# An attention and two-MLP kernel: three elementwise steps change their engine

## The chip, the cores and the metric

One core of one Trainium2 chip runs the kernel. The metric is device microseconds (us) from the first to the last instruction of an execution; lower is better. The engines of a core are TensorE (PE in the profile; PEld is its weight load), VectorE (DVE), ScalarE (ACT), GpSimd (POOL) and SyncE (SP), which here issues the DMAs.

## What is computed

Causal attention with a learned decay, then an MLP with a squared relu, then an MLP with a leaky relu:

```
scores = q @ k.T / 8 + (cum[query] - cum[key]);  masked where key > query
attn   = softmax(scores) @ v            # 4 batches, 8 heads, 576 positions, head size 64
h = x @ w_in   (2304 x 512 @ 512 x 2048)
x1 = (s * relu(h)**2 + b) @ w_out       # first MLP
h2 = x1 @ w_in2
out = max(0.01 * h2, h2) @ w_out2       # second MLP
```

`cum` is the running sum of log f. The weights arrive as float64.

## The kernel before

Products are made in float32r from two halves: an operand is split into a high half, rounded to float32r, and a low half, the rest; three products (high by high, high by low, low by high) replace one. So an MLP block of 128 hidden columns is 12 matmuls of 256 columns for `h` and 12 for the output sums in the first MLP, and 12 and 12 of 512 columns in the second.

The work is staged in nine units of 256 tokens. Units 0 to 7 are a batch's first 256 queries (units 0 to 3, "light" attention: two tiles of queries per head) or its next 256 (units 4 to 7, "heavy": two tiles per head, and a half tile of 64 queries for each pair of heads); unit 8 is the 4 x 64 queries left over. A unit's first MLP runs together with the attention of the next unit, in "slots" laid between its 16 blocks. A prologue makes the first unit's attention and converts the first weights. Then comes the second MLP in five chunks of up to 512 tokens, 16 blocks each; its weights are converted during unit 8 and the first chunk (lines 102 to 106 and 111 to 112: ScalarE, three VectorE steps, ScalarE, GpSimd).

A scheduler turns the program text into one order for each engine; every engine then takes its own instructions strictly in that order, and a waiting instruction holds those behind it. The DMAs that matter here all stand in SP's one queue.

The steps that the change touches:

- **The score of a tile** (`st_score`): two matmuls (four or more for a half tile) into `ps_s`; line 337 on VectorE adds the decays `cumk` (a row of cum, sent by DMA to all partitions, two buffers) and takes the least; line 351 on ScalarE is the exponential. Behind it: line 372 and 373 split the weights into `p_hl` (two buffers), a DMA transposes that to `p_t`, and line 394 multiplies with v.
- **The causal mask** (`st_mask`, line 296): GpSimd writes a large negative number over the diagonal block of `cumk`, after its DMA has landed and before line 337 reads it. It is emitted one tile ahead. Where a light head's two tiles stand side by side, `cumk` is loaded a second time behind itself.
- **g of the first MLP** (`mlp1_g`): line 711 relu, PSUM (`ps_h`, two banks) to SBUF (`graw`), and line 712 square, both ScalarE; line 713 the high half, GpSimd; line 714 the low half, VectorE. The output products (line 733) need both. The bank of `ps_h` is free after line 711.
- **g of the second MLP** (`mlp2_h`): line 798 on ScalarE makes 0.01 h, line 799 on VectorE the maximum with h, line 800 (VectorE) the high half, line 801 (VectorE) the low half. `ps_h` has four banks by then.

## Time and profile before

| | us |
|---|---|
| median of 3 runs | 1104.73 (1100.14 to 1105.5) |
| the profiled execution: span | 1104.1 |
| TensorE busy | 1004.9 (91%) |
| VectorE busy | 710.0 (64%) |
| ScalarE busy | 445.5 (40%) |
| GpSimd busy | 342.0 (31%) |

The profile gives no time for that execution beside its span; the span lies between the lowest and the median run. Matmuls are pipelined, so a TensorE that is busy 91% of the time isn't 91% at its peak: its real load has to be worked out from columns. The shares are averages over stages: the prologue and unit 0 up to about 150 us, units 1 to 6 with attention beside them up to about 600 us, units 7 and 8 up to about 700 us, and the second MLP.

### The profile page before, as it was taken

The numbers are of one execution on the slowest core, as the hardware profiler recorded it, in microseconds if no ns is written. First come the engines' busy times: TensorE is split into PE (matmuls) and PEld (weight loads), VectorE is DVE, ScalarE is ACT, GpSimd is POOL, SyncE is SP. The second block draws the span as 40 slices with busy tenths as digits, with TensorE's granted clock in tenths as the row PEclk, the third lists the DMA queues.
The fourth block names the chain that finished last, engine by engine and source line by source line (L and its number), as shares of the span: only waits on it lengthen the run. The fifth ranks groups of instructions, "written<-read, shape, count | busy, mean of one in ns | idle before, by whom it ended". The sixth has DMA issues, their size and how long they took to land.

```text
span 1104.1 us, 18869 instructions
## 1 busy us (share of the span) xinstructions
PE 1004.9 (91%) x6600; PEld 884.5 (80%) x6600; DVE 710.0 (64%) x1682; ACT 445.5 (40%) x1074; POOL 342.0 (31%) x591
## 2 busy tenths in 40 slices
PE   6876798889899988898989999899999999999998
PEld 4676687888888878787889999767888888888887
DVE  6788977776887877787765159998523533433343
ACT  4555566554555655555554235433101111111111
POOL 4344566644454444454431225433000000000000
PEclk9998989999999999999999999999999999999999
DMA  7388555469898998888874055450200010010010
GB/s 271 125 201 242 154 129 101 98 156 170 171 196 183 211 180 159 197 176 176 187 133 117 8 192 191 124 200 1 77 1 1 20 39 1 1 39 1 0 39 20
DMA packets 191791, 129.32 MB, mean 117 GB/s; under 512 B 137872, under 2 KB 167056, under 8 KB 191696
## 3 DMA queue, kind: packets, MB, share of 16 engines
q1 hardware_dynamic: 191696, 128.12, 48.2%
q8 instruction: 52, 0.85, 0.3%
q14 instruction: 43, 0.35, 0.1%
HBM read 86.58 MB, written 10.04 MB: 88 GB/s over the span
## 4 chain that ended last, share of the span: by engine, by line
PE 47%; DMA 17%; DVE 16%; issue 10%; POOL 6%; ACT 2%; SPq 1%; POOLq 0%; DVEq 0%; ACTq 0%
PE ps_o L809 16%; PE ps_h L791 15%; DMA p_t<-p_hl 7%; PE ps_o L733 6%; PE ps_h L688 6%; DMA cumk<-cumd 4%; DMA qk_raw<-in_qk 3%; DVE wt L104 2%; DVE tt L337 2%; POOL w L112 2%; DVE wt L106 1%; DVE p_hl L373 1%; DVE g L714 1%; POOL g L713 1%; PE ps_v L394 1%
## 5 line engine op out<-in xcount | busy, mean ns | idle before, releaser
L688 PE MATMUL ps_h<-x,w 128*128 128x256 f32 x1728 | 264.3, 288 | 13.2 <-POOL w L112 7.9
L733 PE MATMUL ps_o<-g,w 128*128 128x256 f32 (+1 forms) x1536 | 237.3, 292 | 16.5 <-POOL g L713 9.8
L688 PEld LDWEIGHTS ps_h<-x,w 128*128 128x128 f32 x1728 | 235.1, 194 | 17.1 <-POOL w L112 8.9
L733 PEld LDWEIGHTS ps_o<-g,w 128*128 128x128 f32 x1536 | 206.1, 193 | 27.2 <-POOL g L713 14.3
L809 PE MATMUL ps_o<-w,g 128*128 128x512 f32 x864 | 215.6, 396 | 5.2 <-DVE g L800 3.6
L791 PE MATMUL ps_h<-x,w 128*128 128x512 f32 (+1 forms) x960 | 211.0, 368 | 0.0
L809 PEld LDWEIGHTS ps_o<-w,g 128*128 128x128 f32 x864 | 159.7, 188 | 46.4 <-DVE g L800 6.3
L791 PEld LDWEIGHTS ps_h<-x,w 128*128 128x128 f32 x960 | 169.1, 188 | 32.1
L799 DVE TENSOR_TENSOR t<-ps_h,t 128x512 f32<-128x512 f32 (+1 forms) x80 | 50.8, 635 | 176.7 <-ACT t L798 176.4
L798 ACT ACTIVATE t<-ps_h 128x512 f32<-128x512 f32 (+1 forms) x80 | 44.3, 554 | 279.3 <-PE ps_h L791 279.3
L714 DVE TENSOR_TENSOR g<-graw,g 128x256 fp32r<-128x256 f32 x128 | 70.0, 549 | 66.0 <-POOL g L713 65.9
L351 ACT ACTIVATE tt<-tt,sm 128x512 f32<-128x512 f32 (+4 forms) x128 | 76.8, 600 | 88.3 <-DVE sm L337 79.3
L327 PE MATMUL ps_s<-k_st,q_st 128*128 128x288 f32 (+4 forms) x352 | 91.8, 335 | 20.3 <-DVE sm L337 10.1
L373 DVE SCALAR_TENSOR_TENSOR p_hl<-tt,sm,p_hl 128x512 f16<-128x512 f32 (+4 forms) x128 | 87.5, 692 | 22.5 <-ACT p_hl L372 21.4
L372 ACT ACTIVATE p_hl<-tt,sm 128x512 f16<-128x512 f32 (+4 forms) x128 | 73.5, 596 | 60.3 <-DMA p_t<-p_hl 46.5
L112 POOL TENSOR_TENSOR w<-wt,w 128x512 fp32r<-128x512 f32 x48 | 68.1, 1421 | 79.4 <-ACT w L111 77.8
L296 POOL TENSOR_SCALAR_AFFINE_SELECT cumk<-cumk 128x128 f32<-128x128 f32 (+2 forms) x120 | 46.9, 392 | 137.4 <-DMA cumk<-cumd 99.1
L394 PE MATMUL ps_v<-p_t,v_st 128*128 128x128 f16 (+1 forms) x912 | 60.5, 214 | 27.0 <-DMA p_t<-p_hl 23.8
L327 PEld LDWEIGHTS ps_s<-k_st,q_st 128*128 128x128 f32 x352 | 59.1, 194 | 26.6 <-DVE sm L337 15.1
L713 POOL TENSOR_SCALAR g<-graw 128x256 fp32r<-128x256 f32 x128 | 63.4, 497 | 50.7 <-ACT graw L712 41.1
L337 DVE CUSTOM_DVE_ANT_0 tt<-ps_s,cumk 128x512 f32<-128x512 f32 (+4 forms) x128 | 63.2, 497 | 23.5 <-POOL cumk L296 18.7
L394 PEld LDWEIGHTS <-v_st 128*128 128x128 f16 x912 | 46.8, 100 | 36.7 <-issue 15.8
(88 smaller groups left out, 1116.8 us busy)
## 6 DMA issues: line engine op xcount, KB each, us to landing
w_raw<-in_moe_w_in SPq DMA_DIRECT2D x32, 512.0 KB, 5.4
w_raw<-in_moe_w_out SPq DMA_DIRECT2D x32, 512.0 KB, 5.3
qk_raw<-in_qk SPq DMA_DIRECT2D x32, 480.0 KB, 4.5
cumk<-cumd SPq DMA_DIRECT2D x32, 256.0 KB, 4.3
qk_raw<-in_qk SPq DMA_DIRECT2D x24, 256.0 KB, 3.9
x1d<-x1o SPq DMA_DIRECT2D x36, 128.0 KB, 2.4
cumk<-cumd SPq DMA_DIRECT2D x32, 144.0 KB, 3.5
v_raw<-in_v SPq DMA_DIRECT2D x16, 288.0 KB, 4.2
```

What stands on the lines that cost most here:

```text
L112: nc.gpsimd.tensor_tensor(w[:, 1], x, w[:, 0].bitcast(F32), ALU.subtract)
L327: nc.tensor.matmul(o, q_st[j + e][:, q0 - u0 : q0 - u0 + P], k_st[j + e][:, a, k0 : k0 + kw], start=(e == 0 and a == 0), stop=(e == ne - 1 ...
L337: nc.vector.tensor_tensor_reduce(tt[:, at + k0 : at + k0 + kw], o, cumk[jb][:, at + k0 : at + k0 + kw], scale=-SCALE, scalar=3.0e38 if c = ...
L351: nc.scalar.activation(e, e, AF.Exp, bias=sm[:, r : r + 1], scale=-1.0, accum_out=sm[:, 2 + r : 3 + r])
L373: nc.vector.scalar_tensor_tensor(v[:, 1, :w], e, inv, v[:, 0, :w], ALU.mult, ALU.subtract)
L394: nc.tensor.matmul(av[:, at + e * m : at + (e + 1) * m], v_st[j + e][:, k].rearrange("p l d -> p (l d)"), pt[:, to + l * nk + k, e * m : ( ...
L688: nc.tensor.matmul(ps, wi[:, a, d * P : (d + 1) * P], x[:, c, d], start=(d == 0 and n == 0), stop=(d == ND - 1 and n == 2),)
L713: nc.gpsimd.tensor_scalar(g[:, 0, :UN], raw, 1.0, 0.0, ALU.mult, ALU.add)
L714: nc.vector.tensor_tensor(out=g[:, 1, :UN], in0=raw, in1=g[:, 0, :UN].bitcast(F32), op=ALU.subtract)
L733: nc.tensor.matmul(po[d], wo[:, a, d * P : (d + 1) * P], g[:, c], start=(first and n == 0), stop=(last and n == 2),)
L791: nc.tensor.matmul(ps[:, :n], wi[:, a, d * P : (d + 1) * P], x[:, e, d, :n], start=(d == 0 and k == 0), stop=(d == ND - 1 and k == 2),)
L809: nc.tensor.matmul(po[m], g[:, a, m * P : (m + 1) * P], wo[:, e, :], start=(i == 0 and k == 0), stop=(i == NF - 1 and k == 2),)
```

## The change

Three things are changed together:

- `mlp1_g`: relu and square are done in place in PSUM, and the high half is a ScalarE copy from PSUM. GpSimd has no part in it any more, `graw` is gone, and line 714 (704 after) reads PSUM. The bank of `ps_h` is free only after that.
- the causal mask: an identity matrix times a constant mask block (both bf16, made once in the prologue) is added to the scores by one more matmul per tile (line 317 after). `st_mask` is gone, so is the second load of `cumk` for light heads; `load_cumk(jb + 2)` is emitted behind the tile's line 337.
- `mlp2_h`: leaky relu by one ScalarE activation in place in PSUM, the high half by a ScalarE copy; VectorE keeps the low half, from PSUM.

```diff
-            for at, n in ((0, kend), (kend, P))[: 1 + (u0 == 0)]:
-                nc.sync.dma_start(
-                    out=cumk[jb][rows, at : at + n],
...
+            nc.sync.dma_start(
+                out=cumk[jb][rows, :kend],
...
-    def st_mask(i):
...
+                if end:
+                    nc.tensor.matmul(o[:, kw - m :], ident_h, mask_l if half else mask_h, start=False, stop=True)
                 nc.vector.tensor_tensor_reduce(
                     tt[:, at + k0 : at + k0 + kw],
                     o,
-                    cumk[jb][:, at + k0 : at + k0 + kw],
+                    cumk[jb][:, k0 : k0 + kw],
...
+        if last:
+            load_cumk(jb + 2)
...
-            st_mask(i + 1)
...
+    nc.gpsimd.memset(mask_l, 0.0)
+    for e in range(2):
+        nc.gpsimd.affine_select(
+            out=mask_l[e * D : (e + 1) * D],
...
-        raw = gp.tile([P, UN], F32, tag="raw", name="graw")
...
-        nc.scalar.activation(raw, ps, AF.Relu)
-        nc.scalar.activation(raw, raw, AF.Square)
-        nc.gpsimd.tensor_scalar(g[:, 0, :UN], raw, 1.0, 0.0, ALU.mult, ALU.add)
-        nc.vector.tensor_tensor(out=g[:, 1, :UN], in0=raw, in1=g[:, 0, :UN].bitcast(F32), op=ALU.subtract)
+        nc.scalar.activation(ps, ps, AF.Relu)
+        nc.scalar.activation(ps, ps, AF.Square)
+        nc.scalar.copy(g[:, 0, :UN], ps)
+        nc.vector.tensor_tensor(out=g[:, 1, :UN], in0=ps, in1=g[:, 0, :UN].bitcast(F32), op=ALU.subtract)
...
-        tmp = m2.tile([P, CH], F32, tag="t2", name="t2")
         g = m3.tile([P, 2, CH], F32R, tag="g2", name="g2", bufs=3)
-        raw = tmp[:, :n]
-        nc.scalar.activation(raw, ps[:, :n], AF.Copy, scale=0.01)
-        nc.vector.tensor_tensor(out=raw, in0=ps[:, :n], in1=raw, op=ALU.max)
-        nc.vector.tensor_copy(g[:, 0, :n], raw)
+        raw = ps[:, :n]
+        nc.scalar.activation(raw, raw, AF.Lrelu)
+        nc.scalar.copy(g[:, 0, :n], raw)
         nc.vector.tensor_tensor(out=g[:, 1, :n], in0=raw, in1=g[:, 0, :n].bitcast(F32), op=ALU.subtract)
```

The scheduler moves instructions with it. First GpSimd's queue among the heavy heads (before: L296 is the mask, L713 the high half of g, L242 and L243 split a head's queries, L260 and L371 clear tails, L275 splits v):

```order
L713 TENSOR_SCALAR g<-graw 128x256
L275 TENSOR_SCALAR v_hl<-v_raw,vs 128x5x128
L296 AFFINE_SELECT cumk<-cumk 128x128
L260 MEMSET v_raw 128x64
L296 AFFINE_SELECT cumk<-cumk 128x128
L713 TENSOR_SCALAR g<-graw 128x256
L296 AFFINE_SELECT cumk<-cumk 128x128
L242 TENSOR_SCALAR q_st<-qk_raw 128x384
L243 TENSOR_TENSOR q_st<-qk_raw,q_st 64x384
```

After, in the same stage (L244 and L245 split the queries, L262 and L356 clear tails, L274 and L277 are of v, L409 scales the left-over queries):

```order
L274 TENSOR_SCALAR vs<-vs 128x1
L277 TENSOR_SCALAR v_hl<-v_raw,vs 128x5x128
L244 TENSOR_SCALAR q_st<-qk_raw 128x384
L245 TENSOR_TENSOR q_st<-qk_raw,q_st 64x384
L262 MEMSET v_raw 128x64
L409 TENSOR_SCALAR x_raw<-x_raw,vs 128x64
```

Nothing that a matmul of the first MLP waits for stands in this queue any more, and no instruction in it waits for `cumk`.

Second, TensorE's order of the first MLP beside heavy heads (before: L688 fills `ps_h`, L733 makes the output sums from g, L327 are scores). The g named 4207 is of the `ps_h` named 4194:

```order
L688 MATMUL ps_h_4194<-x_2548,w_1037 128x256
L733 MATMUL ps_o_3535<-g_4139,w_1769 128x256 x6
L733 MATMUL ps_o_3536<-g_4139,w_1769 128x256 x6
L688 MATMUL ps_h_4259<-x_2548,w_1117 128x256 x11
L327 MATMUL ps_s_4750<-k_st_4496,q_st_4495 128x384
L688 MATMUL ps_h_4259<-x_2548,w_1117 128x256
L327 MATMUL ps_s_4750<-k_st_4496,q_st_4495 128x384
L688 MATMUL ps_h_4375<-x_2548,w_1154 128x256 x3
L327 MATMUL ps_s_4819<-k_st_4665,q_st_4664 128x512
L688 MATMUL ps_h_4375<-x_2548,w_1154 128x256
L327 MATMUL ps_s_4819<-k_st_4665,q_st_4664 128x512
L688 MATMUL ps_h_4375<-x_2548,w_1154 128x256 x2
```

After (L680 fills `ps_h`, L724 the output sums, L308 scores, L317 the mask):

```order
L724 MATMUL ps_o_2534<-g_2776,w_1541 128x256 x5
L724 MATMUL ps_o_2535<-g_2776,w_1541 128x256 x5
L680 MATMUL ps_h_2866<-x_1580,w_896 128x256 x12
L724 MATMUL ps_o_2534<-g_2806,w_1634 128x256
L724 MATMUL ps_o_2535<-g_2806,w_1634 128x256
L308 MATMUL ps_s_3588<-k_st_3435,q_st_3434 128x512 x2
L317 LDWEIGHTS ident_h_74
L317 MATMUL ps_s_3588<-mask_h_75,ident_h_74 128x128
L724 MATMUL ps_o_2534<-g_2806,w_1634 128x256 x5
L724 MATMUL ps_o_2535<-g_2806,w_1634 128x256 x5
```

Before, a block of `ps_h` was often begun while two older blocks still lacked their output products; after, blocks of `ps_h` and output products mostly alternate, one block ahead.

Third, ScalarE's queue among heavy heads, before (L711 relu, L712 square, L372 a tile's normalised weights, which wait for the `p_hl` buffer, L351 exponential, L413 output of attention):

```order
L711 ACTIVATE graw_4140<-ps_h_4126 128x256
L712 ACTIVATE graw_4140<-graw_4140 128x256
L372 ACTIVATE p_hl_4469<-tt_4426,sm_4427 128x384
L372 ACTIVATE p_hl_4537<-tt_4483,sm_4484 128x512
L351 ACTIVATE tt_4616,sm_4617<-tt_4616,sm_4617 128x576
L413 COPY x_raw_4326<-ps_v_4401 64x64
```

After (L702 relu, L703 square, L704 the high half, L357 the normalised weights):

```order
L702 ACTIVATE ps_h_5240<-ps_h_5240 128x256
L357 ACTIVATE p_hl_5565<-tt_5522,sm_5523 128x384
L703 ACTIVATE ps_h_5240<-ps_h_5240 128x256
L704 CAST g_5253<-ps_h_5240 128x256
L357 ACTIVATE p_hl_5628<-tt_5579,sm_5580 128x512
L336 ACTIVATE tt_5701,sm_5702<-tt_5701,sm_5702 128x576
```

The high half of g now stands in the queue that also holds the attention's activations, and at this place a wait for a `p_hl` buffer stands between a block's relu and its square.

## Rows read from the trace of the kernel before

The kernel's names in the rows: `g`, `graw`, `ps_h`, `ps_o` are of the MLPs, `ps_s`, `cumk`, `tt`, `sm`, `p_hl`, `p_t`, `ps_v`, `qk_raw` of the attention, `w`, `wt`, `w_raw` of the weights.

**Rows 1.** Windows, all engines: stretch, length, each engine's busy us (instructions), clock, DMA.
```profile
150.00:600.00 450.00, 397.46 (x3464) 374.65 (x3464) 338.92 (x948) 251.74 (x642) 210.24 (x397) 0.97 0.79 163
...
600.00:651.28 51.28, 51.28 (x433) 51.28 (x432) 12.61 (x31) 17.93 (x46) 11.01 (x50) 1.00 0.23 74
...
651.28:763.49 112.21, 104.36 (x581) 86.68 (x579) 107.86 (x153) 51.10 (x96) 51.63 (x44) 1.00 0.46 154
```

**Rows 2.** TensorE by form, 150 to 600 us, first and last of nine.
```profile
L733 PE MATMUL ps_o<-g,w 128*128 128x256 f32 x1152 | 183.3, 294 | 13.9 <-POOL g L713 8.4 <-DVE g L714 4.0 <-DVE x1o L749 0.8
...
L327 PE MATMUL ps_s<-k_st,q_st 128*128 128x256 f32 x22 | 5.2, 294 | 1.1 <-DVE k_st L245 1.1
```

**Rows 3.** Windows, lines 688 and 733 alone, 651.28 to 763.49 us.
```profile
651.28:763.49 112.21, 18.77 (x139) 17.32 (x139) 1.00 0.46 154
...
651.28:763.49 112.21, 24.87 (x170) 21.80 (x168) 1.00 0.46 154
```

**Rows 4.** Waits, 150 to 600 us: us in total, times, longest.
```profile
PE ps_v L394 <- DMA p_t<-p_hl: 20.3, 22, 2.2
PE ps_s L327 <- DVE sm L337: 9.1, 9, 2.4
PE ps_o L733 <- POOL g L713: 8.4, 9, 2.4
PE ps_o L733 <- DVE g L714: 4.0, 9, 0.9
...
DVE g L714 <- POOL g L713: 26.1, 31, 2.3
DVE tt L337 <- POOL cumk L296: 18.4, 17, 3.1
...
POOL cumk L296 <- DMA cumk<-cumd: 85.1, 47, 5.1
...
ACT p_hl L372 <- DMA p_t<-p_hl: 45.1, 37, 3.5
```

**Rows 5.** The chain that ended last, 150 to 600 us, by line.
```profile
by line: DMA p_t<-p_hl 16.9%; issue 13.3%; DMA cumk<-cumd 9.9%; PE ps_o L733 9.0%; DMA qk_raw<-in_qk 6.8%; PE ps_h L688 6.2%; DVE tt L337 4.1%; DVE g L714 3.2%; PE ps_v L394 3.1%; DVE p_hl L373 3.0%; POOL g L713 2.1%; DVE k_st L245 1.9%; PO
```

**Rows 6.** Timeline near 405 us: start, us, instruction, [idle before <- releaser].
```profile
405.26 0.29 POOL L296 TENSOR_SCALAR_AFFINE_SELECT cumk<-cumk 128x128 f32<-128x128 f32 x1 [1.79 <-DMA cumk<-cumd]
...
405.97 0.49 DVE L714 TENSOR_TENSOR g<-graw,g 128x256 fp32r<-128x256 f32 x1 [1.64 <-POOL g L713]
...
405.99 0.50 PE L733 MATMUL ps_o<-g,w 128*128 128x256 f32 x2 [1.47 <-POOL g L713]
```

**Rows 7.** Costs by form: busy us, mean ns of one, idle before.
```profile
L711 ACT ACTIVATE graw<-ps_h 128x256 f32<-128x256 f32 x128 | 47.9, 375 | 54.7 <-PE ps_h L688 34.1 <-DVE g L714 19.0 <-PE ps_s L327 0.5
L798 ACT ACTIVATE t<-ps_h 128x512 f32<-128x512 f32 x64 | 38.2, 597 | 242.2 <-PE ps_h L791 242.2
L549 PE MATMUL ps_s<-misc 128*128 128x128 bf16 x16 | 4.6, 289 | 0.4 <-POOL misc L512 0.4
...
L485 ACT ACT_TABLE_LOAD x1 | 1.3, 1283 | 0.7 <-PEq L906 0.7
```

**Rows 8.** Four VectorE lines: duration ns min/median/max, first and last start.
```profile
L714 DVE TENSOR_TENSOR g<-graw,g x128: 398/426/1547, 150.0 to 696.9; 128x256 fp32r<-128x256 f32 x128
...
L799 DVE TENSOR_TENSOR t<-ps_h,t x80: 414/690/692, 696.3 to 1096.3; 128x512 f32<-128x512 f32 x64, 128x256 f32<-128x256 f32 x16
...
L800 DVE CAST g<-t x80: 293/427/1481, 698.1 to 1096.8; 128x512 fp32r<-128x512 f32 x64, 128x256 fp32r<-128x256 f32 x16
...
L801 DVE TENSOR_TENSOR g<-t,g x80: 424/692/1771, 699.1 to 1097.1; 128x512 fp32r<-128x512 f32 x64, 128x256 fp32r<-128x256 f32 x16
```

**Rows 9.** Timeline near 714 us, GpSimd and VectorE.
```profile
713.61 1.48 POOL L112 TENSOR_TENSOR w<-wt,w 128x512 fp32r<-128x512 f32 x1 [2.47 <-ACT w L111]
...
713.97 1.66 DVE L106 SCALAR_TENSOR_TENSOR wt<-w_raw,wt 128x512 int32<-128x512 int32 x1
```

**Rows 10.** Timeline of GpSimd in the prologue.
```profile
5.40 0.66 POOL L530 TENSOR_SCALAR f_sb<-cum 32x576 f32<-32x576 f32 x1 [4.96 <-DVE cum L525]
```

More of the change, by code (lines that the diff above doesn't have):

```diff
@@ L148, in attention_moe_moe_kernel @@
     bw1 = const.tile([P, ND], F32, name="bw1")
+    ident_h = const.tile([P, P], BF16, name="ident_h")
+    mask_h = const.tile([P, P], BF16, name="mask_h")
+    mask_l = const.tile([P, NL], BF16, name="mask_l")
     mlp1 = ExitStack()
@@ L225, in load_cumk @@
             rows = slice(e * D, (e + 1) * D) if half else slice(0, P)
-            for at, n in ((0, kend), (kend, P))[: 1 + (u0 == 0)]:
-                nc.sync.dma_start(
-                    out=cumk[jb][rows, at : at + n],
-                    in_=cumd[r + e : r + e + 1, :n].to_broadcast([rows.stop - rows.start, n]),
-                )
+            nc.sync.dma_start(
+                out=cumk[jb][rows, :kend],
+                in_=cumd[r + e : r + e + 1, :kend].to_broadcast([rows.stop - rows.start, kend]),
+            )
     def split_head(j):
@@ L284, in split_v @@
             )
-    def st_mask(i):
-        if i >= NTL:
-            return
-        jb, n, ts, last = tiles[i]
-        half = jobs[jb][3]
-        q0, m = QT[ts[0]]
-        for e in range(P // m):
-            diag = cumk[jb][e * m : (e + 1) * m, q0 : q0 + len(ts) * m]
-            nc.gpsimd.affine_select(
-                out=diag,
-                in_=diag,
-                pattern=[[0, len(ts)], [-1, m]],
-                compare_op=ALU.is_ge,
-                fill=MASK,
-                base=0,
-                channel_multiplier=1,
-            )
-        if last:
-            load_cumk(jb + 2)
     def st_score(i):
@@ L324, in st_score @@
                 ne = P // m
+                end = c == len(parts) - 1
                 for e in range(ne):
@@ L331, in st_score @@
                             start=(e == 0 and a == 0),
-                            stop=(e == ne - 1 and a == 1),
+                            stop=(not end and e == ne - 1 and a == 1),
                         )
-                end = c == len(parts) - 1
+                if end:
+                    nc.tensor.matmul(o[:, kw - m :], ident_h, mask_l if half else mask_h, start=False, stop=True)
                 nc.vector.tensor_tensor_reduce(
@@ L509, in attention_moe_moe_kernel @@
         )
-    ident_h = misc[:, P : P + P // 2].bitcast(BF16)
-    mask_h = misc[:, P + P // 2 : 2 * P].bitcast(BF16)
     nc.gpsimd.tensor_copy(ident_h, ident)
@@ L522, in attention_moe_moe_kernel @@
     )
+    nc.gpsimd.memset(mask_l, 0.0)
+    for e in range(2):
+        nc.gpsimd.affine_select(
+            out=mask_l[e * D : (e + 1) * D],
+            in_=mask_l[e * D : (e + 1) * D],
+            pattern=[[-1, NL]],
+            compare_op=ALU.is_ge,
+            fill=MASK,
+            base=0,
+            channel_multiplier=1,
+        )
     nc.vector.tensor_scalar(f_sb, f_sb, 1.0e-4, 1.0, ALU.max, ALU.min)
@@ L631, in attention_moe_moe_kernel @@
             load_cumk(1)
-            st_mask(0)
     slot_no = 0
```

## The prediction

> **What bounds the kernel now.** I read the table of busy times by stretch first, because the shares over the whole span mix stages with different limits. What TensorE can do at best comes from units 7 and 8, from 600 to 651.28 us: 433 matmuls of 256 columns fill the 51.28 us without a gap [rows 1], which is 0.463 ns a column. With that price each stage splits into work and loss.
>
> - 150 to 600 us (units 1 to 6): the nine forms of matmul add up to 781,824 columns (2302 of 256 from the two MLP lines, the rest attention; the first and the last form are in [rows 2]), so 361.7 us of work in 450. Lost: 88.3 us. TensorE is shown busy for 397.5 [rows 1], so only 52.5 us of the loss are open idle time; the rest is refilling after short gaps and stretches at half clock (the mean granted clock is 0.97 here). One us of shown idle time thus goes with 88.3/52.5 = 1.68 us of loss.
> - 651.28 to 763.49 us (end of the first MLP, start of the second, second weights converted): 139 + 170 matmuls of 256 columns [rows 3], and 581 - 309 = 272 of 512, are 218,368 columns or 101.0 us of work in 112.2. Lost: 11.2 us. VectorE is busy for 107.9 of these 112.2 us [rows 1]: it is the bound.
> - After 763 us TensorE has next to no idle time; nothing in this change shortens a matmul, so I expect nothing there.
>
> For the first stage I read the waits next [rows 4]. GpSimd stands 85.1 us, 47 times, before the mask for a `cumk` that has not landed. Its queue is in order, so the high half of g waits behind. The timeline shows one case [rows 6]: the mask waits 1.79 us for `cumk`, VectorE then 1.64 us for GpSimd's half of g, TensorE 1.47 us. In sum VectorE waits 26.1 us for that half and 18.4 for the mask; TensorE's own waits that begin in this knot are 9.1 (scores, for a bank that line 337 frees), 8.4 and 4.0 us (output products). Another 20.3 us are waits for the transposed weights `p_t`. The chain of waits [rows 5] says what would remain: `p_t`, `cumk` and `qk_raw` transfers hold 16.9 + 9.9 + 6.8 = 33.6% of the stretch, and none of these transfers is removed by the change (a light head's second, smaller `cumk` load apart).
>
> **The change, part by part.**
>
> *g of the first MLP.* GpSimd loses its copy, ScalarE gains one of 128 x 256 from PSUM: 375 ns by the nearest row, the relu [rows 7]. That is 96 x 0.375 = 36 us on ScalarE in 150 to 600, which goes from 251.7 to about 288 us of 450: not a bound by load. It removes a handover and, more important, the queue with the mask in it. VectorE's subtraction keeps its count; its median is 426 ns but it has gone up to 1547 [rows 8].
>
> *A lock between GpSimd and VectorE.* At 713.97 us line 106 takes 1.66 us, while GpSimd works on its 1.48 us instruction begun at 713.61 [rows 9]. Line 799, with one operand in PSUM, never takes more than 692 ns, and line 801, the same size with both in SBUF, takes up to 1771 [rows 8]. So an operand in PSUM seems to spare VectorE this. [...] I book no separate gain: the stall can move to the next VectorE instruction with two SBUF inputs.
>
> *What a PSUM operand costs VectorE.* Lines 799 and 801 have the same median, 690 and 692 ns [rows 8]: nothing. [...]
>
> *The mask.* GpSimd loses its 120 selects and the wait before them. Line 337 now waits for the `cumk` transfer itself. TensorE gains 128 matmuls: 112 of 128 columns and 16 of 64. At 0.463 ns a column that is 6.6 + 0.5 = 7.1 us; alone, the same bf16 matmul of the prologue takes 289 ns [rows 7], so 37 us at worst. They stand between other matmuls with both operands ready from the start, so I take 7.1. The prologue gets one memset and two selects for the new mask; they stand ahead of line 530, where GpSimd waits 4.96 us for VectorE [rows 10], and cost nothing while that wait stands. `load_cumk` now comes behind the tile's line 337 instead of the next tile's mask; since the buffer was never free before that line had run, it can't go out much later. What it is moved past in SP's queue, and what then waits behind it (the `p_t` transposes), I bound at 5 us either way: one such landing or so.
>
> *Sum for 150 to 600 us.* Of the knot I take the three waits in full, 9.1 + 8.4 + 4.0 = 21.5 us, and half of the 20.3 for `p_t`, since the instruction that writes `p_hl` stands in the same VectorE queue: 31.7 us. Times 1.68 this is 53 us of loss. The chain's 33.6% of transfers stay, so two thirds go: 35 us. Less 7.1 for the masks: **28 us gained**. Bounds: 0 or a little below if the transfers take over at once (minus the masks, -7), and 88.3 - 7.1 = 81 if nothing is left but matmuls.
>
> *Second MLP.* For each block VectorE loses line 799 (690 ns) and line 800 (427 ns by its median, up to 1481) [rows 8], and ScalarE gains a copy of 128 x 512, 597 ns by line 798 [rows 7]. 272/24 = 11.3 blocks lie in 651.28 to 763.49, so VectorE loses at least 11.3 x 1.12 = 12.6 us and comes down to about 95 us of work. TensorE with 101.0 is then the bound. Of the 11.2 us lost I take **9 gained** (4 to 11). ScalarE has 51 of 112 us there. The leaky relu needs a table load, 1283 ns [rows 7], once; ScalarE waits 242 us for `ps_h` in this MLP [rows 7], so it is covered. In the later chunks ScalarE and VectorE wait for TensorE, so nothing follows.
>
> From 0 to 150 us I book nothing (0 to 4 us of gain: few masks, no split g yet).
>
> 1104.1 - 28 - 9 = 1067 us. The profiled span is within 0.1% of the median, 1104.7, so that serves for both.
>
> **Rivals.**
>
> *Slower: g gets late through ScalarE.* The bank of `ps_h` is now held through three ScalarE instructions and the subtraction, and the new order has blocks and output products alternate. Between the end of a block and its output products TensorE has 24 matmuls of 256 columns (2.84 us) and, by columns, about 1.0 us of attention: 3.84 us. g takes three times about 0.38 and once 0.43: 1.6 us and handovers. The slack is 2.2 us. But ScalarE waits 37 times, up to 3.5 us, for a `p_hl` buffer [rows 4], and its new order has such a wait between relu and square. A wait of 3.5 overruns by 1.3, and block and products both stop: 1.3 x 1.68 = 2.2 us each. If all 37, and as many more brought on by the added copies, did that, 160 us would be lost, against a gain of 37; it turns slower at 17. I expect few: the mean of these waits is 1.2 us. With 20 of them in full, 44 us, the time is 1104 - 37 + 44 = 1111. [...]
>
> *Only the second MLP gains.* The transfers take over in the attention; 150 to 600 us gains some 0 to 15: 1080 to 1095, most likely about 1092. The 33.6% of the chain speaks for it.
>
> *No change to be told:* the masks and the transfers eat the gain, 1099 to 1110.
>
> *Much more:* VectorE's freed time (44.5 us of waits and the lock) speeds up the attention's own chain and the loss falls below half: 1104 - 50 - 11 = about 1040.
>
> **How the numbers follow.** Forecast (1050 to 1085) 0.52; much more (below 1050) 0.13; only the second MLP (1085 to 1098) 0.16; no change 0.08; slower 0.11. Differences under about 0.5% (5.5 us) can't be told from none here. Faster is the sum of the first three: 0.81. The range leaves out the slower cases, part of the unchanged one and the lowest few: 1042 to 1097.
>
> **What would show it.** Right: GpSimd busy about 230 us, no wait for `cumk` in it; line 337 waits for `cumk` under 20 us in all; TensorE's waits for g below 5 us in 150 to 600; VectorE busy under 100 us in the stage where the second MLP starts, and TensorE without gaps there; masks at about 60 ns each. Wrong: waits of `ps_h` matmuls for line 704's or 705's reading of the bank; ScalarE's square or copy late behind line 357; the `p_t` wait of TensorE above 20 us; the mask matmuls with gaps of 0.2 us around them.

## The result and the profile after

| | us, median (range) |
|---|---|
| before | 1102.74 (1100.14 to 1105.5, 4 runs) |
| after | 1089.32 (1084.3 to 1090.52, 4 runs) |
| ratio | 0.9876, 95% interval 0.9844 to 0.9909 |

The change is 1.2% faster: 13.4 us, where 37 were forecast. The first part of the page of the profile after (busy us, share of the span, instructions; span 1088.7 us):

```profile
PE 1013.7 (93%) x6728; PEld 885.8 (81%) x6728; DVE 609.9 (56%) x1522; ACT 525.9 (48%) x1283; POOL 242.0 (22%) x346
```

GpSimd and VectorE have 100 us less each than before, ScalarE 80 more. To see where the time came from, I cut both executions at equal work: the TensorE records give columns, both programs have 1,982,848 of them beside the masks, and the cuts are the columns reached at 150, 600, 690 and 770 us before. Lengths of the five stages in us, up to the start of the last matmul:

| kernel | to 150 | 150 to 600 | 600 to 690 | 690 to 770 | to the end |
|---|---|---|---|---|---|
| before | 150.0 | 450.0 | 90.0 | 80.0 | 329.6 |
| after | 142.6 | 446.9 | 89.3 | 73.9 | 331.6 |
| gained | 7.4 | **3.1** | 0.7 | 6.1 | -2.0 |

The stage booked with 28 us gave 3.1; a loss of 2.0 appeared where nothing was expected. The busy time by stretch of the kernel after, in the stretches that answer to 150 to 600 and 651.28 to 763.49 [rows 1]:

```profile
142.60:589.50 446.90, 405.27 (x3562) 374.86 (x3561) 324.84 (x948) 278.43 (x735) 125.48 (x193) 0.98 0.76 163
640.90:746.20 105.30, 102.73 (x581) 87.42 (x580) 92.49 (x132) 63.20 (x125) 45.55 (x31) 1.00 0.49 165
```

The second stretch is as forecast: VectorE (third) is at 92.49 us of 105.30 and no longer the bound. The first is the puzzle, and its waits (us, times, longest) make it plainer:

```profile
ACT p_hl L357 <- DMA p_t<-p_hl: 76.5, 55, 4.3
ACT tt L336 <- DVE sm L320: 42.8, 50, 1.8
PE ps_v L379 <- DMA p_t<-p_hl: 20.9, 19, 2.8
DVE tt L320 <- DMA cumk<-cumd: 9.7, 12, 1.5
DVE g L705 <- ACT g L704: 7.8, 13, 3.0
PE ps_o L724 <- DVE g L705: 5.0, 9, 1.3
PE ps_s L308 <- DVE sm L320: 2.8, 4, 1.5
PE ps_o L724 <- ACT g L704: 2.2, 5, 0.7
```

The knot of [rows 4] is gone: no GpSimd wait for `cumk`, VectorE's 26.1 us for g's high half are 7.8, its 18.4 for the mask are 9.7 for the transfer, and of TensorE's 21.5 us in the knot 10.0 are left. Yet the stage is hardly shorter. ScalarE's wait for a `p_hl` buffer rose from 45.1 to 76.5, about as much as its wait before the exponential fell, which was 70.1 us:

```profile
ACT tt L351 <- DVE sm L337: 70.1, 63, 2.6
```

So ScalarE comes to the buffer earlier and stands there instead.

### The profile page after: what moved, and what is told of

Its sections match the earlier page's. It is cut to its first block, busy times and chain, and to the rows that moved or that the text cites. A ratio compares the mean times of both kernels' runs of the same rounds, so it can differ in the third digit from the quotient of the medians.

```text
span 1088.7 us, 18609 instructions
## 1 busy us (share of the span) xinstructions
PE 1013.7 (93%) x6728; PEld 885.8 (81%) x6728; DVE 609.9 (56%) x1522; ACT 525.9 (48%) x1283; POOL 242.0 (22%) x346
## 4 chain that ended last, share of the span: by engine, by line
PE 48%; DMA 19%; DVE 16%; issue 7%; POOL 4%; ACT 3%; SPq 2%; POOLq 0%; DVEq 0%; ACTq 0%
PE ps_o L798 16%; PE ps_h L782 15%; DMA p_t<-p_hl 10%; PE ps_o L724 7%; PE ps_h L680 6%; DMA qk_raw<-in_qk 4%; POOL w L112 2%; DVE wt L104 2%; DMA cumk<-cumd 2%; DVE p_hl L358 2%; DVE tt L320 2%; DVE k_st L247 1%; PE ps_v L379 1%; DVE wt L106 1%; PE ps_s L540 1%
## 5 line engine op out<-in xcount | busy, mean ns | idle before, releaser
L680 PE MATMUL ps_h<-x,w 128*128 128x256 f32 x1728 | 248.9, 288 | 5.1 <-POOL w L112 3.1
L724 PE MATMUL ps_o<-g,w 128*128 128x256 f32 (+1 forms) x1536 | 233.7, 294 | 11.5 <-DVE g L705 5.4
L680 PEld LDWEIGHTS ps_h<-x,w 128*128 128x128 f32 x1728 | 224.6, 193 | 7.4 <-POOL w L112 3.6
L724 PEld LDWEIGHTS ps_o<-g,w 128*128 128x128 f32 x1536 | 203.9, 194 | 19.5 <-DVE g L705 9.9
L782 PEld LDWEIGHTS ps_h<-x,w 128*128 128x128 f32 x960 | 169.0, 188 | 34.3
L790 DVE TENSOR_TENSOR g<-ps_h,g 128x512 fp32r<-128x512 f32 (+1 forms) x80 | 51.0, 637 | 258.3 <-ACT g L789 258.2
L798 PEld LDWEIGHTS ps_o<-w,g 128*128 128x128 f32 x864 | 160.4, 188 | 41.6 <-DVE g L790 3.5
L788 ACT ACTIVATE ps_h<-ps_h 128x512 f32<-128x512 f32 (+1 forms) x80 | 43.1, 539 | 250.7 <-PE ps_h L782 250.7
L357 ACT ACTIVATE p_hl<-tt,sm 128x512 f16<-128x512 f32 (+4 forms) x128 | 73.7, 597 | 83.3 <-DMA p_t<-p_hl 76.5
L308 PE MATMUL ps_s<-k_st,q_st 128*128 128x288 f32 (+4 forms) x352 | 84.5, 341 | 10.7 <-DVE sm L320 3.3
L705 DVE TENSOR_TENSOR g<-ps_h,g 128x256 fp32r<-128x256 f32 x128 | 53.3, 418 | 48.1 <-ACT g L704 46.4
L308 PEld LDWEIGHTS ps_s<-k_st,q_st 128*128 128x128 f32 x352 | 55.9, 195 | 15.1 <-POOL q_st L245 4.3
L702 ACT ACTIVATE ps_h<-ps_h 128x256 f32<-128x256 f32 x128 | 47.0, 367 | 37.0 <-PE ps_h L680 36.3
L245 POOL TENSOR_TENSOR q_st<-qk_raw,q_st 64x384 fp32r<-64x384 f32 (+1 forms) x56 | 58.0, 1038 | 4.3
```

The lines of the kernel that those rows point to most:

```text
L245: nc.gpsimd.tensor_tensor(qs[D:, :qn], qr[D:], qs[D:, :qn].bitcast(F32), ALU.subtract)
L308: nc.tensor.matmul(o, q_st[j + e][:, q0 - u0 : q0 - u0 + P], k_st[j + e][:, a, k0 : k0 + kw], start=(e == 0 and a == 0), stop=(not end and ...
L357: nc.scalar.mul(v[:, 0, :w], e, inv)
L680: nc.tensor.matmul(ps, wi[:, a, d * P : (d + 1) * P], x[:, c, d], start=(d == 0 and n == 0), stop=(d == ND - 1 and n == 2),)
L724: nc.tensor.matmul(po[d], wo[:, a, d * P : (d + 1) * P], g[:, c], start=(first and n == 0), stop=(last and n == 2),)
L782: nc.tensor.matmul(ps[:, :n], wi[:, a, d * P : (d + 1) * P], x[:, e, d, :n], start=(d == 0 and k == 0), stop=(d == ND - 1 and k == 2),)
```

## Experiments

### Each part alone, and a third buffer

Theories: LOOP (the attention's own ring sets the stage) and GIVEBACK (g in PSUM returns what the mask gained). `mask_only`, `g_only` and `lrelu_only` each keep one of the three parts and have the old code for the others. Against the changed kernel, `mask_only` is

```diff
...
-        nc.scalar.activation(ps, ps, AF.Relu)
-        nc.scalar.activation(ps, ps, AF.Square)
-        nc.scalar.copy(g[:, 0, :UN], ps)
+        nc.scalar.activation(raw, ps, AF.Relu)
+        nc.scalar.activation(raw, raw, AF.Square)
+        nc.gpsimd.tensor_scalar(g[:, 0, :UN], raw, 1.0, 0.0, ALU.mult, ALU.add)
...
-        nc.scalar.activation(raw, raw, AF.Lrelu)
-        nc.scalar.copy(g[:, 0, :n], raw)
+        nc.scalar.activation(raw, ps[:, :n], AF.Copy, scale=0.01)
+        nc.vector.tensor_tensor(out=raw, in0=ps[:, :n], in1=raw, op=ALU.max)
+        nc.vector.tensor_copy(g[:, 0, :n], raw)
```

`g_only` is the kernel before with the first half of this turned round, `lrelu_only` with the second. `after_hl3`:

```diff
-        ph = ap.tile([P, 10 * P], F16, tag="p_hl", name="p_hl")
+        ph = ap.tile([P, 10 * P], F16, tag="p_hl", name="p_hl", bufs=3)
```

`mask_only`:

> The mask by a matmul alone; both leaky relu and the first MLP's g as before. Two theories of why the stage from 150 to 600 us gave 3 us instead of 28: LOOP, the attention's own ring (split of the weights on ScalarE, transpose by DMA, two buffers each) sets the stage's length, and what GpSimd no longer does only lets ScalarE arrive earlier at a buffer that isn't free; and GIVEBACK, the mask's removal did gain some 15 us there and the g held in PSUM gave it back. LOOP: 8 to 11 us faster than before (the lead of 7 to 8 us that the change had by 150 us, and 0 to 3 more), ratio 0.990 to 0.993. GIVEBACK: 18 us or more faster, ratio 0.984 or less.

Measured 1094.85 us, ratio 0.9912 [0.9887, 0.9938].

`g_only`:

> The first MLP's g in PSUM alone (relu, square and copy by ScalarE, difference by VectorE); mask by GpSimd and leaky relu as before. LOOP: within 3 us of before, ratio 0.997 to 1.003, with TensorE's waits for g gone and its waits for the transposed weights up by as much. GIVEBACK: slower than before by 5 to 12 us, ratio 1.005 to 1.011.

Measured 1118.36 us, ratio 1.0132 [1.0109, 1.0156]: 14.6 us slower, beyond GIVEBACK's range.

`lrelu_only`:

> The second MLP's leaky relu in PSUM alone; all before 650 us as before. Both theories: the lead of 7 us between 690 and 770 us appears here, less the drift of 2 us in the steady second MLP: 4 to 8 us faster, ratio 0.993 to 0.996. If the drift belongs to this part, it shows between 800 and 1080 us.

Measured 1100.86 us, ratio 0.9982 [0.9962, 1.0003]: 2.9 us, less than either theory had and not clear of noise in the whole time; 3.3 in its stage (80.0 to 76.7); no drift.

`after_hl3`:

> The changed kernel with three buffers in place of two for the split weights p_hl, which ScalarE writes and the transposing DMA reads. LOOP: ScalarE's wait of 76.5 us for the transpose to have read a buffer falls under 20, and 8 to 20 us come off the changed kernel's time: 1069 to 1081 us, ratio to before 0.970 to 0.981. GIVEBACK: within 3 us of the changed kernel, 1086 to 1092 us, ratio 0.985 to 0.991.

Measured 1087.69 us, ratio 0.9853 [0.983, 0.9877]: nothing against the change. Its waits in that stage:

```profile
ACT p_hl L357 <- DMA p_t<-p_hl: 62.5, 40, 4.5
PE ps_v L379 <- DMA p_t<-p_hl: 19.5, 16, 2.6
```

The mask run speaks for LOOP, the g run for GIVEBACK, and the third buffer against LOOP (the wait was to fall under 20 us; `p_t` still has two buffers). The parts sum to +2.8 us, the whole is -13.4. Neither theory holds as it stood.

### The change without its g

`mask_lrelu` is the changed kernel with the first half of `mask_only`'s diff alone.

> Mask by a matmul and leaky relu in PSUM, the first MLP's g as before: the changed kernel without its g. The parts alone gave -8.9 us (mask), +14.6 us (g) and -2.9 us (leaky relu), which sum to +2.8 us, but the whole gave -13.4 us, so g in PSUM must cost far less once GpSimd's masks are gone. ADDITIVE for the two parts that don't touch g: -12 us, ratio 0.989 (0.986 to 0.992), and then g in PSUM is worth only 0 to -3 us in the changed kernel. If instead g gains in the changed kernel what it was booked at (it was half of the waits of the knot, 10 us and more), this one stands at -4 us or slower, ratio 0.996 or more.

Measured 1093.57 us, ratio 0.9921 [0.9904, 0.9939]. The two parts add up within 2.5 us, at the edge of ADDITIVE's range; g in PSUM is worth 4 us more in the whole change, and -14.6 alone.

### Fewer transfers

`after_halft` and `before_halft` transpose only the high half of the attention weights (the low halves stay unread, and the output matmul takes the high half twice):

```diff
...
+            high = ph[:, to : to + w]
+            low = ph[:, all_k * P + to : all_k * P + to + w]
...
-            to += 2 * nk * P
+            to += nk * P
...
-                            pt[:, to + l * nk + k, e * m : (e + 1) * m],
+                            pt[:, to + k, e * m : (e + 1) * m],
...
-            to += 2 * nk
+            to += nk
```

> The changed kernel with only the high halves of the attention weights transposed by the DMA; the low halves are computed and stay unread, and the output matmul takes the high half in both of its two products, so the output lacks the low half of the weights while TensorE, ScalarE and VectorE do the same work. Theory QUEUE: the stage from 150 to 600 us is paced by the DMA engines (0.82 to 0.89 busy between 240 and 540 us, 0.42 of their time in 256-byte packets of transposes), so the waits that the change removed came back as later transposes. QUEUE: the DMA share there falls under 0.70, ScalarE's wait for a split buffer from 76.5 to under 30 us, TensorE's wait for transposed weights from 20.9 to under 8 us, and 12 to 25 us come off the changed kernel: 1064 to 1077 us. ENGINES, the rival: the order of ScalarE's and VectorE's own work sets the stage, the DMA shares only look full: less than 5 us off, 1084 to 1090 us.

Measured 1098.05 us, ratio 0.9951 [0.9931, 0.997]: 9 us *slower* than the change. From 240 to 540 us the DMA share (before the last number) fell from 0.86 in the changed kernel to:

```profile
240.00:540.00 300.00, 265.17 (x2357) 241.15 (x2356) 217.63 (x638) 177.21 (x461) 80.36 (x127) 0.98 0.67 150
```

TensorE's wait for `p_t` halved, from 20.9 to 10.4 us, and ScalarE's for a `p_hl` buffer stayed at 72.0.

> The same edit (low halves of the attention weights not transposed) on the kernel before. QUEUE, with the knot of GpSimd's mask and g behind it: gains less than in the changed kernel, since the knot's waits stay: 5 to 12 us faster than before, ratio 0.989 to 0.996, and the difference between the two kernels with this edit opens from 13 us to over 20 us. ENGINES: under 4 us, ratio 0.996 to 1.001, and the difference stays 12 to 15 us.

Measured 1088.14 us, ratio 0.9878 [0.9845, 0.9912]: 15 us faster, and the difference between the two kernels has changed its sign. QUEUE and ENGINES both miss, in both kernels: a DMA share lower by 0.19 went with a slower changed kernel, and one lower by 0.13 (0.89 to 0.76) with a kernel before that is faster by more than QUEUE had. The same edit gave +9 and -15 us, and what differs unasked is the order: of TensorE's 6584 matmuls beside the masks 5404 still start in the order of the changed kernel after this edit. Fewer transfers in a held order weren't tried, so what the transfers are worth isn't shown. From here on the order is held or told.

### g's bank released early

`g_sbuf` is the changed kernel with

```diff
...
-        nc.scalar.activation(ps, ps, AF.Relu)
-        nc.scalar.activation(ps, ps, AF.Square)
-        nc.scalar.copy(g[:, 0, :UN], ps)
+        nc.scalar.activation(raw, ps, AF.Relu)
+        nc.scalar.activation(raw, raw, AF.Square)
+        nc.scalar.copy(g[:, 0, :UN], raw)
```

and VectorE's difference from `raw`.

> The changed kernel, but ScalarE's relu writes a tile in SBUF, and square, copy and difference go on from there: g's bank in PSUM is free again after the relu, as before the change, and ScalarE and VectorE do as many operations as in the changed kernel. Counted in the order in which TensorE's instructions stand, an output block of the first MLP starts with no later hidden block begun 95 times of 143 in the changed kernel, 38 times before, 40 times here. Theory HOLD: the bank that g keeps until VectorE's difference takes away the hidden products with which TensorE covered its waits, and that is where the forecast gain went: 5 to 14 us faster than the changed kernel, 1075 to 1084 us, with TensorE's pauses inside the output sums of 150 to 600 us down by as much. LOOP, the rival (the attention's own ring sets the stage's length whatever g does): within 3 us of the changed kernel, 1086 to 1092 us.

Measured 1082.76 us, ratio 0.9829 [0.9788, 0.9871]: 6.6 us better than the change, 10.4 in the stage. It is in the range of HOLD, but this kernel has an order of its own too.

### The same work in another kernel's order

These kernels get a chain of edges that queue each engine's instructions as another kernel's program has them; an edge orders the issue and waits for nothing else. Masks come right behind their scores. What only one of the two kernels has, GpSimd's masks above all, stands where the scheduler puts it. SP's order is left to the scheduler, and ScalarE's too in `gs_border`, `before_aorder` and `ml_aorder`. In the traces TensorE's common matmuls start in exactly the other kernel's order in all of these runs.

```diff
+    for engine, order in json.loads(zlib.decompress(base64.b64decode(ORDER))).items():
...
+                tc.add_manual_dep(
+                    own[at],
+                    before.name,
+                    mybir.DependencyInfo(mybir.DependencyClass.NoSync, mybir.DependencyReason.DATA),
```

`ml_border`, the work of `mask_lrelu` in the order of the kernel before:

> Mask by a matmul and leaky relu in PSUM, g as before, with the order of TensorE's, ScalarE's, VectorE's and GpSimd's instructions held to that of the kernel before (a mask's matmul right behind its scores). The scheduler that writes the order gives another one after every edit, so a part's own effect and its new order have been mixed so far (this kernel in its own order: 1093.6 us). KNOT, as the prediction had it: with GpSimd's masks and the waits for them gone, the stage from 150 to 600 us is 8 us or more shorter than before in the same order, 1080 to 1087 us in all. LOOP: the stage gives 0 to 4 us, and the rest is 0 to 150 us and the leaky relu: 1090 to 1097 us.

Measured 1075.45 us, ratio 0.9757 [0.9713, 0.9802]: 28.6 us less than the kernel before beside it, better than KNOT's own range. The same work in the order that the scheduler wrote for it took 18 us longer. The waits of `ml_border` in the stage (145 to 575 us):

```profile
PE ps_v L379 <- DMA p_t<-p_hl: 18.6, 21, 2.8
DVE g L706 <- POOL g L705: 12.0, 24, 2.2
DVE tt L320 <- DMA cumk<-cumd: 4.9, 6, 1.3
PE ps_o L725 <- POOL g L705: 2.6, 3, 1.5
PE ps_o L725 <- DVE g L706: 2.6, 4, 1.8
PE ps_s L308 <- DVE sm L320: 1.4, 2, 1.0
```

and of `mask_lrelu`, in its own order (143 to 587 us):

```profile
PE ps_v L379 <- DMA p_t<-p_hl: 25.1, 25, 1.9
DVE g L706 <- POOL g L705: 15.1, 26, 1.5
PE ps_o L725 <- POOL g L705: 10.0, 11, 4.2
PE ps_o L725 <- DVE g L706: 2.6, 5, 0.7
```

Here TensorE's wait for GpSimd's half of g is 10.0 us instead of 2.6, with the same copy on GpSimd in both.

`gs_border`, the work of `g_sbuf`:

> All three parts, with g through ScalarE in SBUF as in the run above, and TensorE's, VectorE's and GpSimd's instructions in the order of the kernel before (ScalarE's order is left to the scheduler, since with the copies on ScalarE the old one can't be kept). KNOT: GpSimd has neither masks nor copies, and the order with which TensorE covered its waits is kept: 1072 to 1082 us. LOOP: 1088 to 1096 us.

Measured 1080.45 us, ratio 0.9805 [0.9768, 0.9842]: in KNOT's range, but 5 us slower than `ml_border`, which leaves g's copy on GpSimd. Against `g_sbuf`, the same work in the scheduler's own order, it is 2.3 us faster in all and 2.7 us longer in the stage (439.2 against 436.5): for this work the scheduler's order isn't the worse one there.

`before_aorder`, the old work in the order of the changed kernel:

> The kernel before, all its operations unchanged, with TensorE's, VectorE's and GpSimd's common instructions in the order of the changed kernel (a mask of GpSimd goes where the scheduler puts it). HOLD: the order of the changed kernel, in which TensorE has a later hidden block begun at only one output block in three, is the worse one: 5 to 15 us slower than before, 1108 to 1118 us, the loss between 150 and 600 us. If the order tells nothing by itself: 1099 to 1106 us.

Measured 1140.67 us, ratio 1.0353 [1.0301, 1.0406]: a loss of 37 us, more than twice what was expected, 29.4 of it from 150 to 600 us and 7.4 from 690 to 770.

### How far an order moves the time by itself

`before_p2` (`after_p8` likewise, with `j == 8`):

```diff
-        vs = ap.tile([P, 5], F32, tag="vs", name="vs", bufs=3)
+        vs = ap.tile([P, 6], F32, tag="vs", name="vs", bufs=3)
...
+        if j == 2:
+            nc.vector.tensor_copy(vs[:, 5:6], vs[:, 3:4])
```

> The kernel before with one more instruction in the whole program: a copy of 128x1 on VectorE at the split of the values of the third head, which nothing reads. Its own time is under 0.1 us, but the scheduler writes another order from there on: 1746 of TensorE's 2885 rows still stand in the common order. Theory ORDER: between two kernels whose orders differ the stage of 150 to 600 us moves by several us whatever the work is; this one ends 3 us or more away from the kernel before, on either side. Rival: an order of the same scheduler is worth the same, and only a change of the work moves the time: within 2.5 us, ratio 0.998 to 1.002.

Measured 1096.2 us, ratio 0.9932 [0.9909, 0.9955]: one idle copy made the kernel 6.6 us faster, through 10.0 us in the stage. That is as theory ORDER has it.

> The changed kernel with one more copy of 128x1 on VectorE, at the values of the ninth head; 2124 of TensorE's 2952 rows stand in the common order. ORDER: 3 us or more away from the changed kernel's 1089.3 us, on either side. Rival: within 2.5 us of it, 1087 to 1092 us.

Measured 1091.96 us, ratio 0.9894 [0.9843, 0.9945]: 2.6 us from the change, inside the rival's range. Theory ORDER is borne out in one of the two.

`ml_aorder`:

> Mask by a matmul and leaky relu in PSUM, g as before, with TensorE's, VectorE's and GpSimd's instructions in the order of the changed kernel. The same operations took 1093.6 us in their own order and 1075.5 us in that of the kernel before. ORDER: the changed kernel's order, written for a g that keeps its bank, is the bad one: 1098 us or more (the kernel before lost 37 us in it, of which GpSimd's masks in places not made for them may be half). Rival, that order costs only because of GpSimd's masks: 1074 to 1090 us.

Measured 1093.57 us, ratio 0.9921 [0.9894, 0.9949]: both theories missed; the changed kernel's order is as good (and as bad) for this work as its own.

`ml_p2order`, the work of `mask_lrelu` in the order of `before_p2`:

> Mask by a matmul and leaky relu in PSUM, g as before, in the order of the kernel before with the one extra copy (that kernel took 1096.2 us). HELD: taking masks and waits out of an order and leaving the order gives 20 to 30 us, whichever order: 1066 to 1077 us. LUCK: the 28.6 us in the order of the kernel before were a chance of that one order; here the gain is under 14 us, 1082 us or more, as the scheduler's own order for these operations gave (9 to 10 us).

Measured 1069.27 us, ratio 0.97 [0.9675, 0.9726]: HELD in all, and the fastest kernel of this study. But of the 26.9 us only 10.5 come in the stage (440.0 to 429.5); 9.2 come before 150 us. TensorE's waits in the knot, in `before_p2` (149 to 590 us):

```profile
PE ps_o L735 <- POOL g L715: 12.0, 15, 1.8
PE ps_o L735 <- DVE g L716: 2.5, 4, 1.2
PE ps_s L329 <- DVE sm L339: 0.7, 2, 0.6
```

and in `ml_p2order` (140 to 570 us):

```profile
PE ps_o L725 <- POOL g L705: 5.1, 6, 2.5
PE ps_o L725 <- DVE g L706: 3.0, 6, 1.0
PE ps_s L308 <- DVE sm L320: 2.9, 4, 1.0
```

`before_mlorder`, the old work in the order of `mask_lrelu`:

> The kernel before, its work unchanged, with TensorE's, ScalarE's, VectorE's and GpSimd's common instructions in the order that the scheduler wrote for mask by matmul with leaky relu in PSUM (that kernel: 1093.6 us). If that order is the worse one whatever the work, by the 18 us that it costs those operations against the order of before: 1115 to 1127 us, the loss between 150 and 600 us. If an order is worth something only for the work that it was written for, and both orders are as good as each other for this work: 1100 to 1108 us.

Measured 1124.46 us, ratio 1.0192 [1.016, 1.0224]: in the range of the first theory, but not in its place. The stage loses 9.1 us, and 9.9 are lost from 690 to 770 us, where the second MLP starts. Its waits (151 to 610 us):

```profile
POOL cumk L296 <- DMA cumk<-cumd: 85.2, 56, 5.5
DVE g L714 <- POOL g L713: 32.2, 37, 3.7
PE ps_o L733 <- POOL g L713: 28.3, 25, 5.6
DVE tt L337 <- POOL cumk L296: 14.2, 13, 2.8
PE ps_v L394 <- DMA p_t<-p_hl: 9.8, 11, 2.1
```

GpSimd waits for `cumk` as long as before (85.1), but TensorE now pays 28.3 us at the output products where it paid 8.4 [rows 4]. Counted in the traces, an output block of the first MLP starts with no hidden block begun beyond the next one 38 times of 144 in the kernel before, 55 times in `mask_lrelu` and 95 times in the changed kernel: less work stands between a g and its use. TensorE's wait for `p_t` is 9.8 us here and was 20.3. Medians of this square, in us:

| work | order of before | of `before_p2` | of `mask_lrelu` | of the changed kernel |
|---|---|---|---|---|
| before | 1102.7 | 1096.2 | 1124.5 | 1140.7 |
| mask and leaky relu | 1075.5 | 1069.3 | 1093.6 | 1093.6 |
| gained by the work | 27.3 | 26.9 | 30.9 | 47.1 |

### The place of the tiles

`before_pad`, and `ml_border_al` with 384 bytes more on `ml_border`:

```diff
+    pad = const.tile([P, 2 * P + NL], BF16, name="pad")
+    nc.gpsimd.memset(pad, 0.0)
```

> The kernel before with 640 bytes a partition of constants that nothing reads, set once at the start: all later tiles lie where those of the changed kernel lie. In the profiles the steady matmuls of the second MLP from 770 us on lose 2 us to the kernel before wherever the mask constants are there (changed kernel, mask alone) and nothing where they aren't (g alone, leaky relu alone). If the place of the tiles does it, this kernel loses 1.5 to 2.5 us between 770 us and its end too; if not, under 0.5 us.

Measured 1104.85 us in one run, in the order of before; its last stage takes 331.5 us where before has 329.6. As expected.

> Mask by a matmul and leaky relu in PSUM in the order of the kernel before, with 384 more bytes a partition of constants that nothing reads, so that later tiles lie 1024 bytes behind their place before the change instead of 640. With 640 bytes the kernel before lost 2.0 us between 770 us and the end in steady matmuls. If it is the place within some 1024 bytes or a smaller power of two, the loss is gone and this kernel is 2 us faster than without the 384 bytes: 1072.5 to 1074.5 us, no drift from 770 us to the end. If any shift costs it: 1075.5 us, drift 2 us.

Measured 1072.56 us, ratio 0.9736 [0.9674, 0.9799]; last stage 329.6 (`ml_border` 331.5). The medians' difference of 2.9 us isn't clear of noise by itself; the stage's is what counts. The busy time of TensorE alone, by stretch (us, busy, number of matmuls, granted clock, DMA share, GB/s), in `before_pad`, then `ml_border`, then `ml_border_al`; the kernel before has 783 there too, the changed one 778:

```profile
820.00:1000.00 180.00, 180.00 (x779) 1.00 0.04 15
```

```profile
820.00:1000.00 180.00, 180.00 (x778) 1.00 0.04 15
```

```profile
820.00:1000.00 180.00, 180.00 (x783) 1.00 0.04 15
```

180 us without a gap are 231.1, 231.4 and 229.9 ns a matmul, at a granted clock of 1.00 in all: it is the place of the tiles, not the clock. Most of it lies in the matmuls into `ps_h`: from one start to the next within a block they take 227.0 ns in the mean in `before` and `ml_border_al`, and 229.8 in `before_pad` and `ml_border`; those into `ps_o` 232.9 and 233.5.

## Why the prediction was half right

**The failed step** is the sum for 150 to 600 us, 28 us of which 3.1 came. All three of its terms failed in the changed kernel. The knot's waits were to go in full, 21.5 us, and 11.5 went. Half of the `p_t` wait was to go, 10.2 us, and it rose by 0.6. And each us of idle time that TensorE loses was to be worth 1.68 us: its idle time fell by 10.9 us (450.0 - 397.5 = 52.5 before [rows 1], 446.9 - 405.3 = 41.6 after), but its busy time rose by 7.8, of which the masks' own price (below) is about 4.1.

What the terms share is that they were read from waits in the old order and booked as if the order stayed, though it was known that the scheduler writes a new one. Held to the old order, mask and leaky relu shorten the stage from 450.0 to 429.3 us, 20.7. The same work takes 443.8 in the order written for it and 447.6 in the order of the changed kernel, so 14.5 or 18.3 go back; with g in PSUM in that last order it is 446.9. In the changed kernel's order the gain is gone whatever does g. The square for the stage alone, in us (the last two columns are taken up under "The terms inside that sum"; the waits are TensorE's three of the knot in [rows 4], for the old work and for the new):

| order of | work of before | mask and leaky relu | gained | TensorE's waits in the knot | 1.68 x waits gone - 4.1 |
|---|---|---|---|---|---|
| before | 450.0 | 429.3 | 20.7 | 21.5 to 6.6 | 20.9 |
| `before_p2` | 440.0 | 429.5 | 10.5 | 15.2 to 11.0 | 3.0 |
| `mask_lrelu` | 459.1 | 443.8 | 15.3 | 33.4 to 13.4 | 29.5 |
| the changed kernel | 479.4 | 447.6 | 31.8 | 26.4 to 11.7 | 20.6 |

That an order moves the time by itself is shown by it: the work gains in each of the four orders, and the orders of `mask_lrelu` and of the changed kernel are slower than that of before for both kinds of work (for the work of before a part of this may be GpSimd's masks, which stand there where the scheduler put them). (Two executions of one order and work differ by 1.5 us in this stage, before and `before_pad`, and by 1.9, `ml_border` and `ml_border_al`; the runs of the kernel before range from 1096.3 to 1107.9 us. 10 to 20 us are not noise, 3 can be.) What isn't shown is that the order is the whole cause. The changed kernel's order was written for a g that keeps its bank, and the two can't be told apart in it. By way of `g_sbuf` the same 3.1 us read otherwise: 20.7, less 9.9 for g through ScalarE in the held order, plus 2.7 for that work's own order, less 10.4 for g in PSUM with the order that comes with it.

**The terms inside that sum.** The knot was real. In the order of before 6.6 us of the 21.5 us of knot waits are left (2.6 + 2.6 + 1.4), 14.9 gone; times 1.68 that is 25.0, less 4.1 for the masks 20.9, and 20.7 were measured, without the further cut to two thirds for the transfers. But that is luck or a property of this one order: in the other three the same sum gives 3.0, 29.5 and 20.6 where 10.5, 15.3 and 31.8 came. Other waits move with the knot's: in the order of `mask_lrelu` TensorE's wait for `p_t` rises from 9.8 to 25.1 us. So a factor from idle time to loss isn't shown, even where the order is held. Of the 35.8 us of loss that the prediction put down to refilling and half clock (88.3 - 52.5), the trace of before has 22.7 us at a granted clock of 0.50, six stretches between 152 and 528 us, which is about 11 us of work; that the rest is refilling was the author's estimate. The half of the `p_t` wait failed there too: 20.3 us are 18.6.

**g through ScalarE** was booked together with the mask, as if both had to leave GpSimd. In the order of before the mask was most of the knot: with it gone, GpSimd's copy of g is late for TensorE by 2.6 us in the stage (10.0 in the order written for `mask_lrelu`), and there is little left to gain. In the held order the move costs 9.9 us of the stage (439.2 against 429.3, with ScalarE's order rewritten). The rival "slower: g gets late through ScalarE" had the right place: alone, with the masks still on GpSimd, that part lost 14.6 us. Whether the bank that g holds in PSUM costs by itself stays open: the sign named for it, `ps_h` matmuls that wait for line 704's or 705's reading, did not show (0.3 us, of a weight load); `g_sbuf` is 10.4 us shorter in the stage, about what an order alone moved the kernel before (10.0); and the changed kernel in the order of before wasn't tried, since with two banks held until VectorE's difference that order can't be kept.

**0 to 150 us**, booked at nothing (0 to 4), gave 7.4, and in the held order 4.8 (`ml_border`) and 8.6 (`ml_border_al`). It is the mask's: alone it gives 9.0 there, the other two parts -1.5 (g) and -1.0. One row that answers to it is TensorE's wait for the weights that GpSimd prepares at line 112, over the whole span 7.9 us before (the idle time at line 688) and 3.1 after (line 680): the masks stood in that queue too.

**The second MLP**, booked at 9 (4 to 11), gave 6.1, in the bounds; leaky relu alone 3.3, in the held order 6.7. The table load that the prediction had for the leaky relu is there after, once, 1283 ns at line 788.

**The masks** are cheaper than 7.1 us. The busy time of a pipelined matmul (230 ns for the row below) is no price; from a mask's start to the next start it is 40 ns in the median of the 128, so 5.1 us, and 4.1 for the 102 that start in the stage; the prediction had all 128 in it.

```profile
L317 PE MATMUL ps_s<-mask_h,ident_h x112: 220/230/330, 45.7 to 555.3; 128*128 128x128 bf16 x112
```

**The operand in PSUM.** Lowest, median and longest duration of the two differences after:

```profile
L705 DVE TENSOR_TENSOR g<-ps_h,g x128: 397/420/426, 140.3 to 681.4; 128x256 fp32r<-128x256 f32 x128
```

```profile
L790 DVE TENSOR_TENSOR g<-ps_h,g x80: 424/692/692, 684.7 to 1082.7; 128x512 fp32r<-128x512 f32 x64, 128x256 fp32r<-128x256 f32 x16
```

Line 714 went up to 1547 ns with both inputs in SBUF and line 801 to 1771 [rows 8]; with one input in PSUM none of 208 is late, though 29 of line 705 and 5 of line 790 start while a GpSimd instruction runs. `g_sbuf`, with ScalarE's copies too but the difference from SBUF, has the late ones again, up to 1510 ns. The lock is in the trace of before: 30 of the 128 of line 714 take over 100 ns more than their median, a GpSimd instruction ran during each, and 26 of them end 0.27 to 0.29 us after it. But two inputs in SBUF aren't needed for it: line 800 has one, and 4 of its 80 are late too, up to 1481 ns [rows 8], each ending 0.28 or 0.29 us after a GpSimd instruction. PSUM costs VectorE nothing that shows: the medians are 420 and 692 ns against 426 and 692.

**Other signs.** GpSimd is busy 242.0 us (230 forecast); TensorE's waits for g are 7.2 us, not under 5; its `p_t` wait is 20.9, just over the 20 named as a sign of error. Of the rivals, "only the second MLP gains" came nearest (1092) with another cause than its transfers, as far as is shown: with the order of before held the stage does gain. The theories of the experiments fell in turn: LOOP by `after_hl3` and `ml_border`, QUEUE by the sign of `after_halft` though not in a held order, HOLD as the whole cause by `ml_border`, whose 18 us against `mask_lrelu` came with g untouched.

**Open.** Why the orders of `mask_lrelu` and of the changed kernel are the worse ones, and how much of the lost gain is order and how much g. The waits place one part at g (10.0 against 2.6 us in `mask_lrelu` and `ml_border`); that the scheduler's own durations make it leave less cover there is a guess. Which engine's order matters wasn't separated, and SP's was never held.

## What to carry to other kernels

Where a scheduler writes the order, a wait in the trace belongs to that order. An edit draws a new one, and here orders alone moved the same work by 24 us (1069.3 to 1093.6) and by 44 (1096.2 to 1140.7), and an idle copy moved the time by 6.6 us in one kernel and by nothing clear of noise in the other. Even in a held order the gain of removing a wait was read well from the trace in one case of four. So measure an edit in the old order as well (the work in both orders, both kinds of work in each), and keep the better order: mask by matmul and leaky relu by ScalarE, in an order that was already there, give 1069.3 us where the whole change gives 1089.3. Of two pieces of work in one in-order queue, move the one that waits: with the mask moved, TensorE's wait for the copy left behind fell from 8.4 to 2.6 us in the same order.

## What was unexpected of the hardware

640 bytes of constants ahead of everything else made float32r matmuls of 512 columns 0.5 to 0.6% slower (231.1 to 231.4 against 229.9 ns), 2.0 us of this kernel; 384 bytes more took it back. What in the place of the tiles does it wasn't looked into.
